# Decoding the second weight in the last batch's first product, and threshold and bias in two instructions

## The chip, the cores and the metric

The kernel runs on one core of a Trainium2 chip. The metric is the time of one execution on the device in microseconds (us), lower is better. The core has five engines that run side by side and wait for each other by semaphores: PE (matmul; its weight loads are shown apart as PEld), DVE (vector), ACT (scalar, activation), POOL (general) and SP, which here only issues DMAs. Each engine takes its instructions in order.

## The reference

Attention over 8 batches, 8 heads, 576 positions and a head width of 64, in which only scores within tau of their row's maximum count, followed by two matrix products with a gate between them:

```
scores = scale * (q @ k.T)                      # 8 x 8 x 576 x 576
thresh = max(scores, rows) - tau
scores = where(scores >= thresh, scores, -1e9)
attn   = exp(scores - max(scores)); attn = attn / (sum(attn) + 1e-9)
x      = (attn @ v) as (4608, 512)
h      = x @ w_in                               # 512 x 2048
g      = h * tanh(softplus(h))
out    = g @ w_out                              # 2048 x 512
```

q, k and v are 32-bit floats; w_in and w_out are 64-bit floats, and the host passes their words as they are. Turning the two 32-bit words of each number into one float32 is done on the chip and is called decoding here.

## The kernel before

**Decoding.** The class Decode (L112 to 146) takes a block of 128 rows and 256 columns. `load` (L121) fetches it with a DMA on SP, 256 KB. `first` (L124) is two ACT instructions that scale the upper and the lower words. `clamp`, `shift` (L131, L134) and the first half of `join` (L137) are three DVE instructions on 128x256 elements, and the second half of `join` is a POOL addition. The decoded number is then split for PE: `upper` (L142) rounds it to PE's fast float format on ACT, and `lower` (L145) subtracts the rounded part from the number, on DVE or POOL. Each weight has 32 such blocks.

**Attention loop.** One loop (L544) runs 288 steps and a few to drain; a step is one block of 128 query rows for one head (or 64 rows each of two heads). Its stages are spread over successive steps: PE computes scores s into PSUM; DVE takes the negated row maximum (`row_max`, L306); DVE computes two columns of the small tile st from it, the threshold st[:,1:2] = -nm - tau/scale and the bias st[:,2:3] = nm*scale (`exponential`, L313); ACT computes e = exp(scale*s + bias); DVE multiplies e by (s >= threshold) into p and sums its rows (`masked`, L322); in the next step POOL divides p by the sum (`normalise`, L337); PE transposes p into tp (and t), ACT copies the transposed block rounded to hi, DVE subtracts to get lo (`lo_main`, L375) and does the same for the short tail (tk); PE multiplies by the values. After every batch of 36 steps the first product's matmuls (`gemm1`, L455) of the batch before are woven into the steps, a listed number of matmuls per step (MIX, L62): each of 32 units is 12 matmuls of 288 columns into one of two PSUM buffers, a copy of the result h to a staging tile hst (by ACT, but by DVE in the last batch), and after every fourth unit a store to DRAM (hd). hst has two buffers. Within the first part of the program all instructions on PE, DVE, ACT and POOL keep the order in which they are written (class InOrder, L78); DMAs on SP and the second product's instructions are placed by the compiler's scheduler.

In `exponential` the first 39 steps (g < JOIN) write threshold and bias with two one-column instructions; from step 39 on they are one `scalar_tensor_tensor` on two columns, with the constant tiles turn and back (L162 to 168):

```
nc.vector.scalar_tensor_tensor(st[:, 1:3], turn, nm, back, ALU.mult, ALU.subtract)
```

Decoding rides in the loop as well (L617). The first weight's 32 blocks start at 12 of every 18 steps and end as split tiles in SBUF. The second weight's 32 blocks (`decode_w2`, L211) follow at 3 of every 18 steps (W2_STEPS); decoded but not split, each goes by a 128 KB DMA to a DRAM tile w2d.

**Last batch and second product.** When the attention's last steps are through, its SBUF is given back and the second part's tiles take its place (L645 on). The last batch's first product (384 matmuls) runs there. Written between its parts, w2d is read back in eight DMAs of 512 KB, ACT rounds each to hi and POOL subtracts to lo (`split_w2`, L674), and the first 256 columns of h are read, gated (`gate`, L666: ACT computes Mish, ACT rounds, POOL subtracts) and split. A part of the first weight's space is given back halfway (L714). Then the second product runs in ten chunks of the 4608 tokens, the first and the last of 256 columns and the rest of 512 (L747): for each chunk and each of four output blocks d, 48 matmuls o from g and the split second weight. The next chunk's h is loaded and gated by ACT and DVE (`make_g`, L730) while PE works on this one. The scheduler may put o matmuls of the first chunk between the last batch's h matmuls.

Of the kernel before, what the change touches and what calls it, by code (L numbers as in the profile page):

```python
# [14 lines left out]
P = 128  # L15
# [3 lines left out]
W1_STEPS = (1, 3, 4, 6, 7, 8, 10, 12, 13, 15, 16, 17)  # L19
W2_STEPS = (0, 12, 16)  # L20
STAGES = ((0, 1, 1), (0, 1, 1), (1, 2, 3))
THIRD = ((),)
# [15 lines left out]
NC = 512  # L38
# [35 lines left out]
def fv(ap):  # L74
    return ap.bitcast(F32)
# [36 lines left out]
class Decode:  # L112
# [24 lines left out]
    def join(self):  # L137
        nc, a, b, c = self.nc, self.a, self.b, self.c
        nc.vector.scalar_tensor_tensor(b, b, 0x80000000, a, ALU.bitwise_and, ALU.bitwise_or)
        nc.gpsimd.tensor_tensor(a, b, c, ALU.add)  # L140

# [7 lines left out]
def attention_moe(tc, q, k, v, tau, w_in, w_out, out):  # L149
# [3 lines left out]
    with ExitStack() as outer:  # L153
# [3 lines left out]
        hd = [dram.tile([P, NF, HB], F32, name=f"hd{i}") for i in range(NBLK)]  # L157
        w2d = dram.tile([P, NF, DM], F32, name="w2d")

        ident = cst.tile([P, P], F32, name="ident")  # L160
        make_identity(nc, ident)
        turn = cst.tile([P, 2], F32, name="turn")  # L162
        back = cst.tile([P, 2], F32, name="back")
        nc.sync.dma_start(back[:, 0:1], tau)
        nc.vector.memset(turn[:, 0:1], -1.0)
        nc.vector.memset(turn[:, 1:2], SCALE)
        nc.vector.memset(back[:, 1:2], 0.0)
        nc.vector.tensor_scalar(back[:, 0:1], back[:, 0:1], 1.0 / SCALE, None, ALU.mult)

        nc = Engines(tc)  # L170
        with ExitStack() as first:
# [6 lines left out]
            with ExitStack() as att:  # L178
# [17 lines left out]
                def decode_w1(d, j):  # L196
# [12 lines left out]
                    return [(work.first, skip), *spread(work, STAGES[(d + j) % 2]), *THIRD, *last]  # L209

                def decode_w2(f, j):  # L211
                    sl = slice(j * WC, (j + 1) * WC)
                    st = dec.tile([P, 4 * WC], U32, name="dec")
                    work = Decode(nc, st, None, None)
                    work.load(w_out[f * P:(f + 1) * P, sl])

                    def last():
                        nc.sync.dma_start(w2d[:, f, sl], fv(work.a))

                    return [(work.first, skip), *spread(work, STAGES[2]), (last,)]  # L220

# [90 lines left out]

                def exponential(s, st, e, apart):  # L313
                    nm = st[:, 0:1]
                    if apart:
                        nc.vector.tensor_scalar(st[:, 2:3], nm, SCALE, None, ALU.mult)
                        nc.vector.tensor_scalar(st[:, 1:2], nm, -1.0, back[:, 0:1], ALU.mult, ALU.subtract)
                    else:
                        nc.vector.scalar_tensor_tensor(st[:, 1:3], turn, nm, back, ALU.mult, ALU.subtract)
                    nc.scalar.activation(e, s[:, :, :HB], AF.Exp, bias=st[:, 2:3], scale=SCALE)  # L320
# [170 lines left out]
                weights = [lambda d=d, j=j: decode_w1(d, j) for j in range(DF // WC) for d in range(ND)]  # L491
                weights += [lambda f=f, j=j: decode_w2(f, j) for f in range(NF) for j in range(DM // WC)]
                decoding = []
# [50 lines left out]
                for g in range(NT + 5):  # L544
# [30 lines left out]
                    if g < NT:  # L575
                        exponential(tiles[g]["s"], tiles[g]["st"], tiles[g]["e"], g < JOIN)
                    if 3 <= g < NT + 3 and not full and ORDER[g % 2] == 1:
# [70 lines left out]

            def halves(pool, d):
                return [pool.tile([P, NF, P], F32R, name=f"w2{n}{d}") for n in "hl"]  # L650

            def slot(pool, shape, kind, n):

                return pool.tile(shape, kind, name="g", tag="g", bufs=n)

            def load_h(ht, c, fs):
# [13 lines left out]

            def load_w2(st, d, fs):
                nc.sync.dma_start(st, w2d[:, fs, d * P:(d + 1) * P])

            def split_w2(st, d, fs):  # L674
                hi, lo = w2[d]
                nc.scalar.copy(hi[:, fs], st)
                nc.gpsimd.tensor_tensor(lo[:, fs], st, fv(hi[:, fs]), ALU.subtract)

            def quarter(k):
                return slice(4 * k, 4 * k + 4)  # L680

            EIGHTS = (slice(0, 8), slice(8, 16))
            n0 = CHUNKS[1]
            w2 = [halves(wr, d) for d in range(2)]
            raw2 = slot(wr, [P, 2, NF, P], F32, 4)
            h0 = slot(wr, [P, NF, n0], F32, 4)
            g0 = [slot(wr, [P, NF, n0], F32R, 4) for _ in "hl"]
            for fs in EIGHTS:
                load_w2(raw2[:, 0, fs], 0, fs)
            for k in range(4):  # L690
                load_h(h0[:, quarter(k)], 0, quarter(k))
            for fs in EIGHTS:
                load_w2(raw2[:, 1, fs], 1, fs)
# [4 lines left out]
            advance(stream, 4 * UNIT)  # L698
            for fs in EIGHTS:
                split_w2(raw2[:, 0, fs], 0, fs)  # L700
            for k in range(4):
                gate(h0[:, quarter(k)], *(g[:, quarter(k)] for g in g0), nc.gpsimd)
            for fs in EIGHTS:
                split_w2(raw2[:, 1, fs], 1, fs)
            advance(stream, 4 * UNIT)
            raw2 = slot(wr, [P, 2, NF, P], F32, 4)
            for d in range(2):
                for fs in EIGHTS:
                    load_w2(raw2[:, d, fs], 2 + d, fs)
            h1 = slot(wr, [P, 8, NC], F32, 4)  # L710
            for k in range(2):
                load_h(h1[:, quarter(k)], 1, quarter(k))
            advance(stream, 8 * UNIT)
            early.close()  # L714
            er = second.enter_context(tc.tile_pool(name="er", bufs=1, side="right"))
            w2.append(halves(er, 2))
            for fs in EIGHTS:
                split_w2(raw2[:, 0, fs], 2, fs)
            for k in range(2):
                nc.scalar.activation(h1[:, quarter(k)], h1[:, quarter(k)], AF.Mish)  # L720
            for _ in stream:
# [3 lines left out]
        nc = tc.nc  # L725
        w2.append(halves(wl, 3))
        for fs in EIGHTS:
            split_w2(raw2[:, 1, fs], 3, fs)

        def make_g(c, q, pool, n):  # L730
            m = CHUNKS[c + 1] - CHUNKS[c]
            pair = slot(pool, [P, 2, 4, NC], F32R, n)
            gh, gl = pair[:, 0, :, :m], pair[:, 1, :, :m]
            for k in range(0, 4, 2):
                fs = slice(4 * q + k, 4 * q + k + 2)
                to = slice(k, k + 2)
                if c == 1 and q < 2:
                    nc.scalar.copy(gh[:, to], h1[:, fs])
                    nc.vector.tensor_tensor(gl[:, to], h1[:, fs], fv(gh[:, to]), ALU.subtract)
                else:  # L740
                    ht = wr.tile([P, 2, NC], F32, name="ht", bufs=2)
                    load_h(ht[:, :, :m], c, fs)
                    gate(ht[:, :, :m], gh[:, to], gl[:, to], nc.vector)
            return gh, gl

        ready = [[[g[:, quarter(q)] for g in g0] for q in range(4)]]
        for c in range(len(CHUNKS) - 1):  # L747
            m = CHUNKS[c + 1] - CHUNKS[c]
            if c + 2 < len(CHUNKS):
                homes = ((wl, 3),) * 3 + ((er, 1),) if c % 2 == 0 else ((wr, 4),) * 4  # L750
                ready.append([make_g(c + 1, q, *homes[q]) for q in range(4)])
            g = ready.pop(0)
            for d in range(ND):
                o = pso.tile([P, NC], F32, name="o")
                n = 0
                for f in range(NF):
                    wh, wlo = w2[d][0][:, f], w2[d][1][:, f]
# [53 lines left out]
```

## Time and profile before

| what | value |
|---|---|
| runs of the kernel | 1437.57, 1447.26 and 1449.11 us, median 1447.26 |
| profiled execution | 1436.91 us |
| its span in the profile | 1435.1 us |
| attention steps, first to last row maximum | 9.6 to 959.0 us |
| last batch's first product, to the second chunk's first matmul | 976.3 to 1054.8 us |
| second product after that | to about 1432 us |

A row of a group in the profile reads: line, engine, operation, output<-inputs, partitions x elements, count, then busy us and mean ns of one, then idle time of the engine ahead of it and what ended it. The line is that of the helper class (L88) for everything issued through InOrder, so instructions are told apart by their tiles. In the view by stretches each row has the stretch, its length, the busy us of each engine with its instruction count in brackets, the granted clock of PE as a share of full speed, the busy share of the DMA engines and GB/s. In the view of the waits a row has who waited for whom, the total us, the number of waits and the longest. In the view in order of time a row has start, length, engine, line, operation and tiles, and in square brackets the idle time ahead. In the views of one tile, three numbers with slashes are the minimum, median and maximum in ns.

### The profile page before, as it was taken

Reading aid. Unit: us, or ns where it says so; the run is one execution under the profiler, and the core shown is the slowest. Engines: PE = TensorE matmul, PEld = TensorE weight load, DVE = VectorE, ACT = ScalarE, POOL = GpSimd, SP = SyncE. Lnnn points to the kernel's source line nnn. Section 1 sums busy time; section 2 is a strip of 40 time slices with the busy share of each in tenths; the row PEclk is TensorE's granted clock in tenths of the full one; section 3 lists DMA queues with packets and bytes.
Section 4 is the critical chain, followed back from the end, with each engine's and each line's share of the span. In section 5 each row is a group of like instructions: output and inputs, shape, how many; then the busy total and the mean of one; then the engine's idle time right before and its main releaser. Section 6 shows DMA issues by size and latency. Waiting matters only on the chain.

```text
span 1435.1 us, 27051 instructions
## 1 busy us (share of the span) xinstructions
PE 1380.3 (96%) x8798; PEld 1228.5 (86%) x8798; DVE 1035.1 (72%) x2730; ACT 936.6 (65%) x2072; POOL 783.7 (55%) x1099
## 2 busy tenths in 40 slices
PE   8998899999999999999999999999999999999999
PEld 5555889899898998989899899998988888888888
DVE  5999999999999999999999999981243322322210
ACT  5888788787887888878788788874255434433310
POOL 4778887778777787877878778756110000000000
PEclk8999999999999999999999999999999999999999
DMA  4334333433333333333333333217545434534210
GB/s 139 100 98 118 116 118 104 139 95 120 114 109 130 104 120 106 112 118 109 122 109 104 97 106 102 92 51 216 181 126 155 138 105 139 137 99 126 87 52 30
DMA packets 134525, 162.98 MB, mean 114 GB/s; under 512 B 23793, under 2 KB 113905, under 8 KB 134385
## 3 DMA queue, kind: packets, MB, share of 16 engines
q1 hardware_dynamic: 134384, 161.26, 37.0%
q8 instruction: 70, 1.15, 0.3%
q14 instruction: 71, 0.57, 0.1%
HBM read 109.84 MB, written 51.38 MB: 112 GB/s over the span
## 4 chain that ended last, share of the span: by engine, by line
PE 68%; DVE 18%; ACT 5%; issue 5%; DMA 2%; POOL 1%; SPq 1%; DVEq 0%; ACTq 0%; POOLq 0%
PE o L760 26%; PE h L88 16%; PE s L88 11%; PE y L88 10%; DVE st L88 7%; PE tp L88 5%; DVE p L88 5%; DVE dec L88 2%; ACT e L88 2%; DVE lo L88 2%; DVE tk L88 1%; PE t L88 1%; DMA hd<-hst 1%; POOL g L88 1%; ACT x L88 1%
## 5 line engine op out<-in xcount | busy, mean ns | idle before, releaser
L760 PE MATMUL o<-g,w2h 128*128 128x512 f32 (+1 forms) x1280 | 365.0, 370 | 0.9 <-DVE g L669 0.7
L88 PE MATMUL h<-xh,w1h 128*128 128x288 f32 x1024 | 303.7, 297 | 3.3 <-DVE hst L88 2.4
L88 PE MATMUL h<-xl,w1h 128*128 128x288 f32 x1024 | 303.4, 296 | 0.5 <-POOL xl L88 0.5
L88 PE MATMUL h<-xh,w1l 128*128 128x288 f32 x1024 | 303.3, 296 | 0.0
L88 PE MATMUL s<-k,q 128*128 128x288 f32 (+1 forms) x1280 | 259.4, 328 | 41.7 <-DVE p L88 37.8
L88 ACT ACTIVATE e<-s,st 128x576 f32<-128x576 f32 x288 | 214.0, 743 | 128.5 <-DVE st L88 125.8
L88 POOL TENSOR_SCALAR p<-p,st 128x576 f32<-128x576 f32 x288 | 245.3, 852 | 75.2 <-DVE st L88 56.2
L760 PEld LDWEIGHTS o<-g,w2h 128*128 128x128 f32 x1280 | 231.9, 188 | 44.8 <-DVE g L669 1.1
L88 PEld LDWEIGHTS s<-k,q 128*128 128x128 f32 (+1 forms) x1280 | 183.9, 191 | 94.9 <-DVE p L88 74.8
L88 DVE SCALAR_TENSOR_TENSOR p<-s,st,e 128x576 f32<-128x576 f32 x288 | 234.8, 815 | 30.3 <-ACT e L88 24.6
L760 PE MATMUL o<-g,w2l 128*128 128x512 f32 (+1 forms) x640 | 236.7, 370 | 0.0
L88 DVE TENSOR_REDUCE st<-s 128x1 f32<-128x576 f32 x288 | 216.3, 751 | 7.3 <-PE s L88 7.2
L88 PEld LDWEIGHTS h<-xh,w1h 128*128 128x128 f32 x1024 | 193.8, 189 | 4.0 <-DVE hst L88 2.8
L88 PEld LDWEIGHTS h<-xl,w1h 128*128 128x128 f32 x1024 | 193.9, 189 | 0.7 <-POOL xl L88 0.7
L88 PEld LDWEIGHTS h<-xh,w1l 128*128 128x128 f32 x1024 | 193.6, 189 | 0.0
L669 DVE TENSOR_TENSOR g<-ht,g 128x1024 fp32r<-128x1024 f32 (+1 forms) x68 | 78.4, 1162 | 155.6 <-ACT g L668 155.6
L88 DVE TENSOR_TENSOR lo<-tp,hi 128x512 fp32r<-128x512 f32 (+1 forms) x280 | 171.2, 620 | 13.8 <-ACT hi L88 13.1
L88 PE MATMUL tp<-ident,p 128*128 128x128 f32 x1152 | 174.9, 274 | 3.8 <-DVE lo L88 1.3
L88 ACT CAST hi<-tp 128x512 fp32r<-128x512 f32 (+1 forms) x280 | 150.5, 548 | 16.3 <-PE tp L88 12.9
L667 ACT ACTIVATE ht<-ht 128x1024 f32<-128x1024 f32 (+1 forms) x68 | 68.7, 1010 | 132.1 <-DMA ht<-hd 128.6
L88 PEld LDWEIGHTS tp<-ident,p 128*128 128x128 f32 x1152 | 138.8, 141 | 13.9 <-issue 6.9
L88 POOL TENSOR_TENSOR x<-x,yo 64x256 f32<-64x256 f32 (+1 forms) x112 | 90.2, 806 | 89.8 <-ACT yo L88 88.0
(64 smaller groups left out, 2265.0 us busy)
## 6 DMA issues: line engine op xcount, KB each, us to landing
hd<-hst SPq DMA_DIRECT2D x64, 576.0 KB, 3.3
r<-q SPq DMA_DIRECT2D x120, 160.0 KB, 2.3
r<-k SPq DMA_DIRECT2D x120, 160.0 KB, 2.3
ht<-hd SPq DMA_DIRECT2D x60, 288.0 KB, 3.3
r<-v SPq DMA_DIRECT2D x56, 160.0 KB, 2.3
dec<-w_in SPq DMA_DIRECT2D x32, 256.0 KB, 2.8
dec<-w_out SPq DMA_DIRECT2D x32, 256.0 KB, 2.8
out_t<-ost SPq DMA_DIRECT2D x32, 256.0 KB, 2.8
```

What stands on the lines that cost most here:

```text
L88: made = method(*args, **kwargs)
L667: nc.scalar.activation(ht, ht, AF.Mish)
L669: engine.tensor_tensor(gl, ht, fv(gh), ALU.subtract)
L760: nc.tensor.matmul(o[:, :m], a, b, start=n == 0, stop=n == 3 * NF - 1)
```

## The change

The second weight is no longer decoded in the attention loop, and w2d is gone. Its 32 blocks are fetched, decoded and split in the last batch's stage, one step of a small pipeline ahead of each of the 32 units of 12 matmuls: at unit u, ACT's `first` of block u-3; ACT's `upper` of block u-5; DVE's `clamp`, `shift` and `sign` and POOL's `add` (the two halves of `join`) of block u-4; and `lower` of block u-5, on DVE for odd blocks and on POOL for even ones, after which the buffer fetches block u+1. There are six buffers, four in a slot of the large tiles and two that the second product later uses for h. The split weight is held as two halves of 256 output columns instead of four of 128. The first chunk's four gates come at units 9, 11, 13 and 15. The second chunk's h, of which half was loaded and put through Mish in this stage, is loaded at unit 18 and gated wholly in `make_g`. The tiles for g are four slots each in two pools, in place of three, one and four in three pools.

In the loop, threshold and bias are two one-column instructions in every step, the bias first; the tile turn and the second column of back go.

```diff
-W2_STEPS = (0, 12, 16)
...
     def join(self):
-        nc.vector.scalar_tensor_tensor(b, b, 0x80000000, a, ALU.bitwise_and, ALU.bitwise_or)
-        nc.gpsimd.tensor_tensor(a, b, c, ALU.add)
+        self.sign()
+        self.add()
...
-                def exponential(s, st, e, apart):
+                def exponential(s, st, e):
                     nm = st[:, 0:1]
-                    if apart:
-                        nc.vector.tensor_scalar(st[:, 2:3], nm, SCALE, None, ALU.mult)
-                        nc.vector.tensor_scalar(st[:, 1:2], nm, -1.0, back[:, 0:1], ALU.mult, ALU.subtract)
-                    else:
-                        nc.vector.scalar_tensor_tensor(st[:, 1:3], turn, nm, back, ALU.mult, ALU.subtract)
+                    nc.vector.tensor_scalar(st[:, 2:3], nm, SCALE, None, ALU.mult)
+                    nc.vector.tensor_scalar(st[:, 1:2], nm, -1.0, back, ALU.mult, ALU.subtract)
...
-                weights += [lambda f=f, j=j: decode_w2(f, j) for f in range(NF) for j in range(DM // WC)]
...
-                    if weights and (g % 18 in W1_STEPS if len(weights) > 32 else g % 18 in W2_STEPS):
+                    if weights and g % 18 in W1_STEPS:
...
+            def fetch(i):
+                if i < 2 * NF:
+                    st = four[:, i % 6] if i % 6 < 4 else small(U32, [P, 4 * WC])
+                    work[i] = Decode(nc, st, None, None)
+                    j, f = divmod(i, NF)
+                    work[i].load(w_out[f * P:(f + 1) * P, j * WC:(j + 1) * WC])
+
+            def decode_step(u):
+
+                if (i := u - 3) in work:
+                    work[i].first()
+                if (i := u - 5) in work:
+                    j, f = divmod(i, NF)
+                    work[i].hi, work[i].lo = (w[:, f] for w in w2[j])
+                    work[i].upper()
+                if (i := u - 4) in work:
+                    work[i].clamp()
+                    work[i].shift()
+                    work[i].sign()
+                    work[i].add()
+                if (i := u - 5) in work:
+                    work.pop(i).lower(nc.vector if i % 2 else nc.gpsimd)
+                    fetch(i + 6)
...
+            for u in range(NF * 2):
+                if u == NF + 2:
+                    early.close()
+                    er = second.enter_context(tc.tile_pool(name="er", bufs=1, side="right"))
+                    w2.append(weights2(er, 1))
+                decode_step(u)
+                if u in (9, 11, 13, 15):
+                    k = (u - 9) // 2
+                    gate(h0[:, quarter(k)], *(g[:, quarter(k)] for g in g0), nc.gpsimd)
+                if u == NF + 2:
+                    h1 = slot(wr, [P, 8, NC], F32, 4)
+                    for k in range(2):
+                        load_h(h1[:, quarter(k)], 1, quarter(k))
+                advance(stream, UNIT)
+            for u in range(NF * 2, NF * 2 + 5):
+                decode_step(u)
```

More of the change, by code (lines that the diff above doesn't have):

```diff
@@ L19 @@
 W1_STEPS = (1, 3, 4, 6, 7, 8, 10, 12, 13, 15, 16, 17)
-W2_STEPS = (0, 12, 16)
-STAGES = ((0, 1, 1), (0, 1, 1), (1, 2, 3))
+STAGES = ((0, 1, 1), (0, 1, 1))
 THIRD = ((),)
@@ L137, in join, with sign, add @@
     def join(self):
-        nc, a, b, c = self.nc, self.a, self.b, self.c
-        nc.vector.scalar_tensor_tensor(b, b, 0x80000000, a, ALU.bitwise_and, ALU.bitwise_or)
-        nc.gpsimd.tensor_tensor(a, b, c, ALU.add)
+        self.sign()
+        self.add()
+    def sign(self):
+        self.nc.vector.scalar_tensor_tensor(self.b, self.b, 0x80000000, self.a, ALU.bitwise_and, ALU.bitwise_or)
+    def add(self):
+        self.nc.gpsimd.tensor_tensor(self.a, self.b, self.c, ALU.add)
     def upper(self):
@@ L157, in attention_moe @@
         hd = [dram.tile([P, NF, HB], F32, name=f"hd{i}") for i in range(NBLK)]
-        w2d = dram.tile([P, NF, DM], F32, name="w2d")
         ident = cst.tile([P, P], F32, name="ident")
         make_identity(nc, ident)
[L162 to L168, printed above, removed]
+        back = cst.tile([P, 1], F32, name="back")
+        nc.sync.dma_start(back, tau)
+        nc.vector.tensor_scalar(back, back, 1.0 / SCALE, None, ALU.mult)
         nc = Engines(tc)
@@ L209, in decode_w1 @@
                     return [(work.first, skip), *spread(work, STAGES[(d + j) % 2]), *THIRD, *last]
[L211 to L220, printed above, removed]
                 def prep(pi):
@@ L575, in attention_moe @@
                     if g < NT:
-                        exponential(tiles[g]["s"], tiles[g]["st"], tiles[g]["e"], g < JOIN)
+                        exponential(tiles[g]["s"], tiles[g]["st"], tiles[g]["e"])
                     if 3 <= g < NT + 3 and not full and ORDER[g % 2] == 1:
@@ L647, in attention_moe, with small @@
             pso = second.enter_context(tc.tile_pool(name="pso", bufs=4, space=PSUM))
-            def halves(pool, d):
-                return [pool.tile([P, NF, P], F32R, name=f"w2{n}{d}") for n in "hl"]
             def slot(pool, shape, kind, n):
                 return pool.tile(shape, kind, name="g", tag="g", bufs=n)
+            def small(kind, shape):
+                return wr.tile(shape, kind, name="ht", tag="ht", bufs=2)
             def load_h(ht, c, fs):
@@ L669, in gate, with weights2 @@
                 engine.tensor_tensor(gl, ht, fv(gh), ALU.subtract)
[L671 to L677, printed above, removed]
             def quarter(k):
                 return slice(4 * k, 4 * k + 4)
-            EIGHTS = (slice(0, 8), slice(8, 16))
+            def weights2(pool, j):
+                return [pool.tile([P, NF, WC], F32R, name=f"w2{n}{j}") for n in "hl"]
             n0 = CHUNKS[1]
-            w2 = [halves(wr, d) for d in range(2)]
-            raw2 = slot(wr, [P, 2, NF, P], F32, 4)
+            w2 = [weights2(wr, 0)]
+            four = slot(wr, [P, 4, 4 * WC], U32, 4)
             h0 = slot(wr, [P, NF, n0], F32, 4)
             g0 = [slot(wr, [P, NF, n0], F32R, 4) for _ in "hl"]
-            for fs in EIGHTS:
-                load_w2(raw2[:, 0, fs], 0, fs)
+            work = {}
+            def fetch(i):
[19 more added lines that the diff above has]
+                    fetch(i + 6)
+            for i in range(6):
+                fetch(i)
             for k in range(4):
                 load_h(h0[:, quarter(k)], 0, quarter(k))
-            for fs in EIGHTS:
-                load_w2(raw2[:, 1, fs], 1, fs)
             for _ in stream:
@@ L697, in attention_moe @@
             UNIT = 12
[L698 to L720, printed above, removed]
+            for u in range(NF * 2):
[14 more added lines that the diff above has]
+                decode_step(u)
             for _ in stream:
@@ L725, in attention_moe, with make_g @@
         nc = tc.nc
[L726 to L730, printed above, removed]
+        def make_g(c, q, pool):
             m = CHUNKS[c + 1] - CHUNKS[c]
-            pair = slot(pool, [P, 2, 4, NC], F32R, n)
+            pair = slot(pool, [P, 2, 4, NC], F32R, 4)
             gh, gl = pair[:, 0, :, :m], pair[:, 1, :, :m]
@@ L737, in make_g @@
                 if c == 1 and q < 2:
-                    nc.scalar.copy(gh[:, to], h1[:, fs])
-                    nc.vector.tensor_tensor(gl[:, to], h1[:, fs], fv(gh[:, to]), ALU.subtract)
+                    gate(h1[:, fs], gh[:, to], gl[:, to], nc.vector)
                 else:
-                    ht = wr.tile([P, 2, NC], F32, name="ht", bufs=2)
+                    ht = small(F32, [P, 2, NC])
                     load_h(ht[:, :, :m], c, fs)
@@ L749, in attention_moe @@
             if c + 2 < len(CHUNKS):
-                homes = ((wl, 3),) * 3 + ((er, 1),) if c % 2 == 0 else ((wr, 4),) * 4
-                ready.append([make_g(c + 1, q, *homes[q]) for q in range(4)])
+                ready.append([make_g(c + 1, q, (wl, wr)[c % 2]) for q in range(4)])
             g = ready.pop(0)
@@ L755, in attention_moe @@
                 n = 0
+                j, at = divmod(d * P, WC)
                 for f in range(NF):
-                    wh, wlo = w2[d][0][:, f], w2[d][1][:, f]
+                    wh, wlo = (w[:, f, at:at + P] for w in w2[j])
                     gh, gl = (x[:, f % 4] for x in g[f // 4])
```

## The prediction

> **What bounds the kernel now.** I read the page first, then the stretches, then the waits inside them. The page:
>
> ```profile
> span 1435.1 us, 27051 instructions
> PE 1380.3 (96%) x8798; PEld 1228.5 (86%) x8798; DVE 1035.1 (72%) x2730; ACT 936.6 (65%) x2072; POOL 783.7 (55%) x1099
> PE 68%; DVE 18%; ACT 5%; issue 5%; DMA 2%; POOL 1%; SPq 1%; DVEq 0%; ACTq 0%; POOLq 0%
> ```
>
> PE looks full everywhere, but the chain of waits gives DVE 18% of the span, so somewhere PE waits for DVE. The stores of the decoded second weight say where its decode lies:
>
> ```profile
> L218 SPq DMA_DIRECT2D w2d<-dec x32: 326/327/425, 208.2 to 820.5; - x32
> ```
>
> I cut the span by that. The view by stretches, for tile e alone, has one ACT instruction per attention step, so its second count (behind ACT's busy time) is the number of steps. The fence after it is the same view for all engines, in the order PE, weight loads, DVE, ACT, POOL, then clock, DMA share and GB/s:
>
> ```profile
> 126.60:186.20 59.60, 12.42 (x32) 11.16 (x15) 0.91 0.40 116
> 186.20:849.70 663.50, 162.97 (x396) 147.22 (x198) 1.00 0.36 113
> 849.70:959.00 109.30, 28.84 (x71) 26.04 (x35) 1.00 0.26 85
> ```
>
> ```profile
> 186.20:849.70 663.50, 633.09 (x4668) 602.81 (x4667) 638.69 (x1727) 535.72 (x1319) 526.32 (x782) 1.00 0.36 113
> 849.70:959.00 109.30, 108.93 (x832) 106.85 (x831) 103.28 (x290) 89.97 (x216) 80.86 (x125) 1.00 0.26 85
> 976.30:1054.80 78.50, 75.36 (x567) 74.54 (x568) 23.52 (x39) 29.39 (x28) 30.98 (x14) 0.98 0.60 185
> ```
>
> A step takes 663.5/198 = 3.351 us while the second weight is decoded and 109.3/35 = 3.123 us just after, with the same matmuls per step (4668/198 = 23.6, 832/35 = 23.8). PE idles 4.6% of the first stretch and 0.3% of the second. What the weight loads wait for, in the same two stretches:
>
> ```profile
> PEld s L88 <- DVE p L88: 58.2, 119, 1.1
> ...
> PEld s L88 <- DVE p L88: 2.2, 8, 0.4
> ```
>
> Taking these waits out gives (663.5 - 58.2)/198 = 3.057 and (109.3 - 2.2)/35 = 3.060. So a step that never waits for DVE would cost PE 3.06 us; DVE bounds the stretch with decode, PE nearly bounds the one without. After the attention the last batch's product runs on PE alone with DVE, ACT and POOL mostly idle (last row).
>
> **Threshold and bias.** The group that goes, with its mean in ns, and the spread (minimum, median, maximum in ns) of it and of the two one-column forms, which the kernel has in its first steps:
>
> ```profile
> L88 DVE SCALAR_TENSOR_TENSOR st<-turn,st,back 128x2 f32<-128x2 f32 x249 | 119.4, 479 | 0.0
> ...
> L88 DVE SCALAR_TENSOR_TENSOR st<-turn,st,back x249: 210/368/926, 127.4 to 959.8; 128x2 f32<-128x2 f32 x125
> L88 DVE TENSOR_SCALAR st<-st x381: 134/144/155, 10.4 to 961.8; 128x1 f32<-128x1 f32 x191
> L88 DVE TENSOR_SCALAR st<-st,back x39: 201/204/207, 10.5 to 124.3; 128x1 f32<-128x1 f32 x39
> ```
>
> Two columns cost 479 ns on average but 210 at best, so most of it is a stall. The instructions in order of time show on what:
>
> ```profile
> 859.54 0.87 POOL L88 TENSOR_TENSOR x<-x,yo 64x320 f32<-64x320 f32 x1 [1.40 <-ACT yo L88]
> 860.06 0.37 DVE L88 SCALAR_TENSOR_TENSOR st<-turn,st,back 128x2 f32<-128x2 f32 x1
> ...
> 861.66 0.83 POOL L88 TENSOR_SCALAR p<-p,st 128x576 f32<-128x576 f32 x1
> 862.84 0.22 DVE L88 SCALAR_TENSOR_TENSOR st<-turn,st,back 128x2 f32<-128x2 f32 x1
> ```
>
> The first ends at 860.43 with POOL's instruction (860.41); the second, with POOL idle since 862.49, takes 0.22. The one-column forms never exceed 155 and 207 ns in 381 and 39 cases, so they don't stall so. The pair is 144 + 204 = 348 ns against 479, a gain of 0.13 us a step, 33 us over 249 steps if DVE were the bound throughout. DVE instructions also overlap their neighbours by some 0.08 (below, the reduce lasts until 81.07 and the next begins at 80.99), short ones most: two sums and the pair together take 81.30 - 80.99 = 0.31.
>
> ```profile
> 80.32 0.75 DVE L88 TENSOR_REDUCE st<-s 128x1 f32<-128x576 f32 x1
> 80.99 0.27 DVE L88 TENSOR_SCALAR st<-st 128x1 f32<-128x1 f32 x3
> 81.30 0.15 DVE L88 RECIPROCAL st<-st 128x1 f32<-128x1 f32 x1
> ```
>
> That puts the pair near 0.18 and the gain near 0.2. As a range for the edit: a loss of 0.14 (0.35 - 0.21) if the stall only moves to a neighbour, to a gain of 0.2; nearest is the case of the first steps, where the pair stands in the same place, so I take the gain. The bias also comes first, so e on ACT starts earlier.
>
> [...]
>
> **The second weight out of the loop.** What one decode costs each engine in the loop, from the groups by line:
>
> ```profile
> L88 DVE TENSOR_SCALAR dec<-dec 128x256 f32<-128x256 f32 x64 | 33.1, 518 | 0.0
> L88 DVE TENSOR_SCALAR dec<-dec 128x256 uint32<-128x256 uint32 x64 | 25.1, 392 | 0.5
> L88 DVE SCALAR_TENSOR_TENSOR dec<-dec 128x256 uint32<-128x256 uint32 x64 | 44.7, 698 | 0.7
> L88 ACT ACTIVATE dec<-dec 128x256 uint32<-128x256 uint32 x64 | 28.1, 439 | 0.0
> L88 POOL TENSOR_TENSOR dec<-dec 128x256 uint32<-128x256 uint32 x64 | 48.0, 751 | 2.3 <-DVE dec L88 1.4
> L88 POOL TENSOR_TENSOR w1l<-dec,w1h 128x256 fp32r<-128x256 f32 x23 | 17.5, 763 | 2.9 <-ACT w1h L88 2.6
> ```
>
> Per decode the loop loses 0.52 + 0.39 + 0.70 = 1.61 us on DVE, two ACT instructions of 0.44, 0.75 on POOL, and on SP a load and a store. 32 x 1.61 = 51 us of DVE plus the 33 above is 84 us, but PE allows no step under 3.06. So the loop can fall to between 3.06 and 3.123 us; I take 3.09, as PE's work varies from step to step. Terms: 198 x (3.351 - 3.09) = 51.7; 35 x (3.123 - 3.09) = 1.2; and in the 15 steps before 186.2, where the first weight still keeps DVE busy, 15 x 0.2 = 3. **Loop: -56 us**, between -45 (3.123, nothing else) and -63 (3.06 in 233 steps and the 3).
>
> **The same work in the last batch.** Before, the stage runs from the last batch's first h matmul to the first 512-column o, the 78.5 us from 976.3 to 1054.8 in the third row above. Its pace, its first load, and what the moved work costs when nothing stalls it (minimum first):
>
> ```profile
> 1021.03 0.46 DVE L88 COPY hst<-h 128x288 f32<-128x288 f32 x1 [1.14 <-PE h L88]
> 1040.20 0.46 DVE L88 COPY hst<-h 128x288 f32<-128x288 f32 x1 [1.14 <-PE h L88]
> 1041.00:1051.00 10.00, 10.00 (x87) 10.00 (x86) 1.00 0.23 85
> 977.96 1.00 SPq L672 DMA_DIRECT2D g<-w2d  x2
> dec<-w_out SPq DMA_DIRECT2D x32, 256.0 KB, 2.8
> L88 POOL TENSOR_TENSOR g<-g 128x1024 fp32r<-128x1024 f32 x4 | 9.4, 2394 | 1.3 <-ACT g L88 1.3
> L88 DVE TENSOR_SCALAR dec<-dec x128: 272/386/966, 24.0 to 813.3; 128x256 f32<-128x256 f32 x64, 128x256 uint32<-128x256 uint32 x64
> L88 DVE SCALAR_TENSOR_TENSOR dec<-dec x64: 414/710/2307, 26.9 to 817.4; 128x256 uint32<-128x256 uint32 x64
> L88 DVE TENSOR_TENSOR w1l<-dec,w1h x9: 409/412/956, 50.9 to 141.0; 128x256 fp32r<-128x256 f32 x9
> ```
>
> PE needs (1040.20 - 1021.03)/12 = 1.60 us per unit of 12 matmuls, 51 us for 32 units, and 10/87, about 0.12 us, for each of the first chunk's 192 o matmuls (23 us). Now every unit also carries one decode, ahead of the copy of h on DVE, which is in order: a late decode holds the copy, the copy holds one of two PSUM buffers, and PE stops. DVE alone would need, at the short durations 0.27 + 0.27 + 0.41 and half of 0.41, plus 0.46 for the copy, 1.6 us: just PE's pace. But the stalls above tie DVE's SBUF instructions to POOL's. If one runs at a time, a pair of units holds 4 x 0.27 + 2 x 0.41 + 0.41 on DVE and 2 x 0.75 + 0.76 on POOL, 4.6 us, less some overlap, about 4.3; the copies from PSUM hide under POOL. So 2.15 us per unit, and four gate subtractions on POOL (2.39 each) add 9.6.
>
> [...]
>
> The stage's first load can issue when the attention's buffers are free (977.96), lands 2.8 later, ACT converts (0.87), so decoding starts about 6.5 us into the stage. Unit 31 carries decode 27: 6.5 + 28 x 2.15 + 9.6 = 76.3; the last four decodes end under the 23 us of o matmuls that follow, some 3 us of which fit into the gaps before. 76.3 + 23 - 3 = 96.3 against 78.5: **+18 us**. Bounds: PE's pace 1.6 and no gaps, 51 + 23 + 2 = 76, so -2; and nothing side by side, (4.6 + 0.92)/2 = 2.8 per unit, 6.5 + 78 + 9.6 + 23 = 117, so +39. Chunk 1's gates, later on ACT than before, I put at +2. The stores to and loads from w2d, the POOL splits and their waits go, but they lay beside PE's work, and I count them as nothing; if uncovered they would add at most the 3 us by which 78.5 exceeds PE's 75.4.
>
> **Sum.** The profiled execution took 1436.9, 1.8 beyond its span. 1436.9 - 56 + 18 + 2 = 1401. The three runs shown lie between 1437.57 and 1449.11 with the median 10 above the profiled one; I add half of that: **1406 us**.
>
> **Rivals.** (1) The last batch hides the decode: +0 for +18 and +2; 1436.9 - 56 + 5 = 1386. For it: DVE 30% busy there now. Against it: the stalls. 13%. (2) Two instructions cost more than one and the stall moves on: +0.14 on DVE a step. The stretch without decode then goes to 3.123 + 0.14 = 3.26, the loop gains 198 x 0.09 - 50 x 0.14 = 11, and 1436.9 - 11 + 20 + 5 = 1451, no change. For it: 210 ns at best. Against it: 155 ns at most for a one-column form. [...] 10%. (3) The loop ends between, near 3.2, because with less work in front of it p waits for e: 198 x 0.15 + 3 = 33, 1436.9 - 33 + 20 + 5 = 1429. For it: such waits exist; against it: they are small, and e now starts earlier. 12%.
>
> ```profile
> DVE p L88 <- ACT e L88: 24.6, 85, 1.4
> ```
>
> (4) Slower: in the last batch SP is one queue for loads of the weight and stores of h. A load waits until its buffer's decode is done, the store behind it waits too, and h's two staging buffers stop DVE, which stops the decode. DVE has such waits now:
>
> ```profile
> DVE hst L88 <- DMA hd<-hst: 15.2, 2, 8.3
> ```
>
> With 7 waits of 8.3 us it costs 58 more: 1401 + 58 + 5 = 1464; it decides from 5 us per store (36 in all). Against it: loads are six decodes ahead, 13 us against 2.8. 7%.
>
> **Chances and range.** My case 58%, with its own range 1388 to 1424; rivals as given. The bounds of the terms span 1436.9 - 63 - 2 = 1372 to 1436.9 - 45 + 41 = 1433. Range 1383 to 1436: it takes in (1) and (3), cuts the corner where every term is at its best, and leaves out (2) and (4). Measurements of this kernel tell about 1% from no change: 58 + 13 + most of (3) make faster 0.82, (2) and the rest same 0.11, (4) slower 0.07.
>
> **What would show it.** Steps of 3.06 to 3.12 us from 186 on, PE's waits for DVE p under 10 us; the one-column pair at 143 and 204 ns; the last batch's copies of h some 2.2 us apart instead of 1.6, DVE and POOL stalled in turn, the stage near 96 us. Wrong: steps above 3.2 (2 or 3), copies at 1.6 (1), or h's copies waiting for stores (4).

## The result, and the profile after

The changed kernel took 1400.47 us (median of 4 runs, 1396.20 to 1407.83) against 1442.41 us for the kernel before (4 runs, 1435.35 to 1449.11). The ratio is 0.9715, with a 95% interval of 0.9644 to 0.9786: faster by 2.9%, some 41 us. Executions of one kernel lie up to 14 us apart here. The profiled execution took 1407.83 us, the slowest of the four. The lines of its page that answer to those shown for the kernel before:

```profile
span 1406.0 us, 27557 instructions
PE 1370.3 (97%) x8798; PEld 1234.7 (88%) x8798; DVE 1008.2 (72%) x2992; ACT 947.1 (67%) x2098; POOL 774.1 (55%) x1107
PE 88%; DVE 5%; ACT 3%; DMA 2%; issue 2%; POOL 0%; SPq 0%; POOLq 0%; ACTq 0%; DVEq 0%
```

PE's share of the busy time moved from 96% to 97%, which says little. The chain of waits says more: PE went from 68% to 88% of the span, DVE from 18% to 5%. The view by stretches, cut at the same steps as before: first for tile e (the second count is the number of steps), then for all engines.

```profile
134.80:195.20 60.40, 12.42 (x32) 11.18 (x15) 0.92 0.35 104
195.20:803.70 608.50, 163.22 (x396) 147.54 (x198) 1.00 0.33 103
803.70:911.40 107.70, 28.88 (x72) 26.07 (x35) 1.00 0.27 87
```

```profile
195.20:803.70 608.50, 608.42 (x4667) 599.97 (x4668) 560.30 (x1829) 520.06 (x1252) 496.52 (x749) 1.00 0.33 103
803.70:911.40 107.70, 107.69 (x835) 106.83 (x833) 99.66 (x327) 89.94 (x216) 80.95 (x125) 1.00 0.27 87
928.70:1026.40 97.70, 83.31 (x567) 80.67 (x568) 79.82 (x153) 55.07 (x118) 50.65 (x54) 0.91 0.62 199
```

A step of the 198 now takes 608.5/198 = 3.073 us and PE is busy in all of it; in the 35 after them it takes 3.077. The waits of PE's weight loads for p, in the same two stretches, were 58.2 and 2.2 us:

```profile
PEld s L87 <- DVE p L87: 8.7, 34, 1.9
...
PEld s L87 <- DVE p L87: 0.8, 4, 0.2
```

Where the 29.1 us between the two profiled spans lie, stretch by stretch:

| stretch | before | after | difference | forecast |
|---|---|---|---|---|
| up to step 39 | 126.6 | 134.8 | +8.2 | 0 |
| 15 steps with the last of the first weight | 59.6 | 60.4 | +0.8 | -3 |
| 198 steps | 663.5 | 608.5 | -55.0 | -51.7 |
| 35 steps | 109.3 | 107.7 | -1.6 | -1.2 |
| last row maximum to the start of the last batch's stage | 17.3 | 17.3 | 0 | 0 |
| the last batch's stage | 78.5 | 97.7 | +19.2 | +18 |
| rest of the second product | 380.3 | 379.6 | -0.7 | +2 |

The first 39 steps are written the same in both kernels. Their difference belongs to the execution: PE's granted clock in the first 50 us was 0.90 in the one and 0.76 in the other (rows in the last section), and in the kernels of the experiments that share these steps they ended between 125.9 us (clock 0.93) and 138.4 us (0.66). Without the first row the difference is 37.3 us.

A note on the cut of the stage: the h matmul at 976.3 is not the last batch's first. Nine h matmuls of it stand up to 2.3 us earlier, ahead of a wait for the last xh. The cut lies at the same matmul in every kernel here, so the differences hold.

### The profile page after: what moved, and what is told of

It reads as the page before. It is cut to its first block, busy times and chain, and to the rows that moved or that the text cites. A ratio compares the mean times of both kernels' runs of the same rounds, so it can differ in the third digit from the quotient of the medians.

```text
span 1406.0 us, 27557 instructions
## 1 busy us (share of the span) xinstructions
PE 1370.3 (97%) x8798; PEld 1234.7 (88%) x8798; DVE 1008.2 (72%) x2992; ACT 947.1 (67%) x2098; POOL 774.1 (55%) x1107
## 4 chain that ended last, share of the span: by engine, by line
PE 88%; DVE 5%; ACT 3%; DMA 2%; issue 2%; POOL 0%; SPq 0%; POOLq 0%; ACTq 0%; DVEq 0%
PE o L751 27%; PE h L87 25%; PE s L87 14%; PE y L87 12%; PE tp L87 9%; PE t L87 1%; DVE g L87 1%; DVE st L87 1%; DVE p L87 1%; DVE ht L87 1%; DVE dec L87 1%; DMA g<-hd 1%; DMA g<-w_out 1%; ACT e L87 1%; DVE hst L87 0%
## 5 line engine op out<-in xcount | busy, mean ns | idle before, releaser
L87 ACT ACTIVATE e<-s,st 128x576 f32<-128x576 f32 x288 | 214.4, 744 | 36.1 <-DVE st L87 29.0
L87 DVE TENSOR_TENSOR lo<-tp,hi 128x512 fp32r<-128x512 f32 (+1 forms) x280 | 174.7, 632 | 50.7 <-ACT hi L87 43.8
L751 PEld LDWEIGHTS o<-g,w2l 128*128 128x128 f32 x640 | 121.9, 191 | 25.9 <-POOL w2l L87 3.9
```

Of the source, the lines that this page charges most:

```text
L87: made = method(*args, **kwargs)
```

## The experiments

Times are ratios to the kernel before on the same chip, with 95% intervals; stages are from each one's profile, from that h matmul to the first 512-column o. A stage is one execution: the same code of the stage took 97.7 us in the changed kernel, and 96.4 and 95.2 us in the two experiments that leave it as it is. Differences of up to some 2.5 us between two stages show nothing by themselves.

**Moving the decode alone.** The changed kernel with the two-column instruction from step 39 on, as before.

```diff
+                    if apart:
                         nc.vector.tensor_scalar(st[:, 2:3], nm, SCALE, None, ALU.mult)
                         nc.vector.tensor_scalar(st[:, 1:2], nm, -1.0, back[:, 0:1], ALU.mult, ALU.subtract)
+                    else:
+                        nc.vector.scalar_tensor_tensor(st[:, 1:3], turn, nm, back, ALU.mult, ALU.subtract)
```

> The decode of the second weight is moved as in the change, but threshold and bias stay one two-column instruction from step 39 on. Theory (PE's own 3.06 us per step is the bound once the decode is out of the loop, the two-column instruction only adds what its stalls make PE wait): steps as in the stretch without decode of the kernel before, 3.12 us, against 3.077 in the changed kernel, so 233 x 0.045 = 10 us slower than the changed kernel and about 28 us faster than before; the last batch's stage 97 to 98 us as in the changed kernel. Rival (DVE is still the bound and every stall of that instruction is paid, 0.2 us a step): steps 3.28, 46 us slower than the changed kernel, slower than before.

Measured: 1414.69 us, ratio 0.9832 (0.9789 to 0.9876). The 198 and 35 steps, by tile e, and the stage:

```profile
185.30:805.90 620.60, 163.46 (x396) 147.19 (x198) 1.00 0.33 101
805.90:915.10 109.20, 28.82 (x71) 26.03 (x35) 1.00 0.26 85
...
932.40:1028.80 96.40, 81.03 (x567) 78.00 (x568) 79.86 (x153) 55.13 (x119) 50.64 (x54) 0.95 0.61 200
```

Steps of 620.6/198 = 3.134 us, near the 3.123 of the stretch without decode before, and the stage about as long as in the changed kernel. The theory holds: DVE no longer adds its whole stall to a step, and the two-column instruction costs 0.06 us a step. The move by itself is worth 1.7%.

**Two instructions alone.** The kernel before with the two one-column instructions in every step; the decode stays in the loop.

```diff
-                    if apart:
...
-                    else:
-                        nc.vector.scalar_tensor_tensor(st[:, 1:3], turn, nm, back, ALU.mult, ALU.subtract)
```

> Only threshold and bias become two one-column instructions; the second weight is decoded in the loop as before. Theory (DVE bounds the steps with decode, and the pair takes about 0.2 us a step off it; PE's 3.06 is the floor): steps with decode 3.351 - 0.2 = 3.15, those without 3.08, so 198 x 0.2 + 35 x 0.04 = 41 us less in the loop and nothing more in the last batch: 36 to 41 us faster than before, as much as the whole change. Rival (the decode itself, not the two-column instruction, is what makes PE wait): the loop gains only the 0.045 us a step that the stretch without decode gained, 10 us.

Measured: 1405.85 us, ratio 0.9757 (0.9722 to 0.9792). By tile e, the stage, and the wait of PE's weight loads in the 198 steps:

```profile
197.40:824.80 627.40, 163.04 (x396) 147.20 (x198) 1.00 0.38 119
824.80:932.40 107.60, 28.87 (x72) 26.06 (x35) 1.00 0.27 87
...
949.70:1027.20 77.50, 73.50 (x568) 72.88 (x569) 23.41 (x39) 29.31 (x28) 31.04 (x14) 1.00 0.60 187
...
PEld s L88 <- DVE p L88: 22.4, 79, 0.7
```

Steps with decode take 627.4/198 = 3.169 us: 0.18 less than before, near the 0.2 of the theory. Not all of it need be DVE's own time. In these steps DVE waited 11.7 us for e in the kernel before and not at all here, as the bias no longer comes out of a stalled instruction (its waits for hi rose from 3.5 to 16.8 us). How much that makes of the 36.1 us was not tried apart. Most of the gain needs no move of the decode. Given the two instructions, the move takes 627.4 - 608.5 = 18.9 us out of the loop and adds 97.7 - 77.5 = 20.2 us to the last batch; the intervals of this kernel and of the whole change overlap. The gains don't add: the move alone gives 1.7%, the pair alone 2.4%, both 2.9%, because both take DVE time out of the same steps, and together they come to 3.07 us, where PE is busy all the time.

**One two-column instruction with one tensor input.** The changed kernel, with threshold and bias together again, but not as a two-tensor instruction.

```diff
-                    nc.vector.tensor_scalar(st[:, 2:3], nm, SCALE, None, ALU.mult)
-                    nc.vector.tensor_scalar(st[:, 1:2], nm, -1.0, back, ALU.mult, ALU.subtract)
+                    nc.vector.tensor_scalar(st[:, 1:3], turn, nm, back, ALU.mult, ALU.subtract)
```

> The changed kernel with threshold and bias in one instruction again, two columns, but with a single SBUF tensor as input and both other operands as per-partition scalars (the bias is lower by the same constant in every row, which the division by the sum takes out). Theory (the two-column instruction stalled because it has two tensor inputs in SBUF): about 0.2 us without stalls, steps 3.07 to 3.08, as the changed kernel. [...]

Measured: 1426.06 us, ratio 0.9896 (0.9856 to 0.9936). The group, its spread, and the 198 steps by tile e:

```profile
L87 DVE TENSOR_SCALAR st<-turn,st,back 128x2 f32<-128x2 f32 x288 | 132.8, 461 | 0.0
...
L87 DVE TENSOR_SCALAR st<-turn,st,back x288: 279/377/1649, 9.4 to 932.8; 128x2 f32<-128x2 f32 x144
...
199.30:822.70 623.40, 163.42 (x395) 147.31 (x198) 1.00 0.32 101
...
301.77 0.83 POOL L87 TENSOR_SCALAR p<-p,st 128x576 f32<-128x576 f32 x1
302.21 0.41 DVE L87 TENSOR_SCALAR st<-turn,st,back 128x2 f32<-128x2 f32 x1
...
949.40:1044.60 95.20, 81.85 (x567) 79.21 (x568) 79.83 (x153) 54.94 (x118) 50.67 (x54) 0.93 0.61 199
```

The theory falls: the instruction stalls as the one with two tensor inputs did (461 ns on average against 479), and steps take 3.148 us instead of 3.07 to 3.08. The two rows in order of time show it end with POOL's instruction (302.62 and 302.60). Counted over the traces, 162 of its 288 took over 320 ns, and each of these ended within 60 ns of a POOL instruction; of the kernel before's 249, 146 took over 300 ns, and 145 of them ended so. The changed kernel's 918 one-column instructions on st never took more than 209 ns, though POOL was at work when more than 740 of them began.

So the stall doesn't need the second tensor input, and in these kernels the one-column instructions avoid it. Instructions with two SBUF inputs were held as well: of the kernel before's 64 sign instructions of the decode, which have two, 50 took over 450 ns, and all 50 ended 265 to 286 ns after a POOL instruction. Whether two columns or two tensor inputs held the two-column instruction in the kernel before is not shown, and no run shows why one column escapes.

The steps after the first weight are not the whole loss. These 233 steps take 16.5 us more than in the changed kernel, but the time is 26 us longer. The first 39 steps have the instruction here too (435 ns on average) and ended at 138.2 us; how much of that is the instruction and how much the start's clock, 0.80 in the first 50 us, the run doesn't show.

**Subtractions to DVE in the last batch.**

```diff
-                    work.pop(i).lower(nc.vector if i % 2 else nc.gpsimd)
+                    work.pop(i).lower(nc.vector)
...
-                    gate(h0[:, quarter(k)], *(g[:, quarter(k)] for g in g0), nc.gpsimd)
+                    gate(h0[:, quarter(k)], *(g[:, quarter(k)] for g in g0), nc.vector)
```

> The changed kernel, but in the last batch all 32 subtractions of lower and the four of the gates go to DVE, which does them in 0.41 and 1.22 us against POOL's 0.76 and 2.40. Theory (DVE's and POOL's SBUF instructions exclude each other, so what counts is their sum): per pair of units 0.35 us less, 16 x 0.35 = 6, and 4 x 1.2 = 5 for the gates: the stage 87 us instead of 97.8, the kernel 10 us faster than the changed one. Rival (DVE alone is the bound there, POOL runs beside it): DVE gets 16 x 0.41 + 4 x 1.22 = 11 us more, the stage 109 us.

Measured: 1395.03 us, ratio 0.9685 (0.9647 to 0.9724); the stage

```profile
928.80:1017.10 88.30, 79.81 (x567) 76.42 (x568) 69.94 (x171) 53.73 (x117) 27.18 (x34) 0.96 0.64 212
...
990.60 0.45 DVE L87 COPY hst<-h 128x288 f32<-128x288 f32 x1
992.49 0.45 DVE L87 COPY hst<-h 128x288 f32<-128x288 f32 x1
```

88.3 us, 7 to 9 less than the three executions with these subtractions on POOL, as the theory of exclusion has it, and far from the rival's 109. DVE got 18 instructions more and was busy 69.9 us instead of 79.8: the same 96 instructions of clamp, shift and sign took 54.2 us in the changed kernel and 38.1 here, as fewer POOL instructions stood in their way. A unit in the steady part takes 1.89 us. In the whole time the gain can't be told: the interval of the ratio overlaps with that of the changed kernel.

**All decode instructions to DVE.** On top of the kernel before this one.

```diff
-                    work[i].add()
+                    nc.vector.tensor_tensor(work[i].a, work[i].b, work[i].c, ALU.add)
```

> [...] POOL does nothing in the last batch's stage. Theory (exclusion): DVE has 0.2 + 0.2 + 0.34 + 0.34 + 0.34 + 0.46 = 1.9 us per unit and waits for no one, the clamp and shift always take 0.27 us: units of 1.9, the gates 1.2 each, the stage 84 to 86 us. Rival (DVE alone is the bound): 32 x 0.4 us more than the kernel with lower and gates on DVE, the stage 13 us longer than there.

Measured: 1391.39 us, ratio 0.9655 (0.9611 to 0.9699). One unit of DVE in order of time, and the stage:

```profile
984.70 0.45 DVE L87 COPY hst<-h 128x288 f32<-128x288 f32 x1
985.07 0.61 DVE L87 TENSOR_SCALAR g<-g 128x256 f32<-128x256 f32 x2
985.72 0.42 DVE L87 SCALAR_TENSOR_TENSOR g<-g 128x256 uint32<-128x256 uint32 x1
986.17 0.43 DVE L87 CUSTOM_DVE_ANT_0 g<-g 128x512 uint16<-128x512 uint16 x1
986.52 0.42 DVE L87 TENSOR_TENSOR w2l<-g,w2h 128x256 fp32r<-128x256 f32 x1
986.85 0.45 DVE L87 COPY hst<-h 128x288 f32<-128x288 f32 x1
...
925.80:1007.00 81.20, 75.37 (x553) 73.31 (x553) 68.47 (x190) 47.21 (x110) 1.53 (x2) 0.98 0.64 214
```

The decode's DVE instructions stall no more: clamp and shift take 0.61 together, and each of the 64 took 280 to 297 ns. The addition runs as a custom instruction on 512 half-words, here of 0.43 us. The unit is 2.15 us, not 1.9, longer than the 1.89 of the kernel before this one, and still the stage is shorter, 81.2 us. The rows count 553 matmuls here and 567 there: the first 512-column o now comes ahead of the first chunk's last 14 matmuls, so the like stage is some 1.7 us longer, about 82.9 (14 at 0.12 us, an estimate from the rate of o matmuls before).

The stage thus isn't set by the unit alone. The last h matmul starts 73.4 us into the stage there and 73.9 here, but counted in order of time, 122 instead of 91 of the first chunk's o matmuls now stand ahead of it, where PE would idle, and fewer remain behind it. Both theory and rival missed that. That this count decides is not shown: the spread kernel below has only 67 ahead and a stage no longer than that with 91.

**Gates spread over ACT; everything one unit earlier; then all of it on DVE.** Three kernels, each on top of the one with the subtractions on DVE: Mish and rounding of a gate in successive units; also every decode one unit earlier; also the addition on DVE.

```diff
+                if u in (9, 11, 13, 15):
+                    k = (u - 9) // 2
+                    nc.scalar.activation(h0[:, quarter(k)], h0[:, quarter(k)], AF.Mish)
+                if u in (10, 12, 14, 16):
+                    k = (u - 10) // 2
+                    nc.scalar.copy(g0[0][:, quarter(k)], h0[:, quarter(k)])
+                    nc.vector.tensor_tensor(g0[1][:, quarter(k)], h0[:, quarter(k)], fv(g0[0][:, quarter(k)]), ALU.subtract)
...
-                if (i := u - 3) in work:
+                if (i := u - 2) in work:
...
-                if (i := u - 4) in work:
+                if (i := u - 3) in work:
```

> The kernel with lower and gates on DVE, and each gate's rounding and subtraction one unit after its Mish, so that ACT's work is spread over eight units. Theory (in the four gate units ACT sets the pace: 0.87 + 0.40 + 1.06 + 1.05 = 3.4 us, and the waits behind it make 4.2): units 9 to 16 take 2.4 each on average instead of 3.0, 4 to 5 us less in the stage, 83 to 84 us against 88.3. Rival (those units wait for the loads of h and for the store of h, not for ACT): no change.

> As the kernel with spread gates, and every decode one unit earlier: first of block u-2, clamp to add of block u-3, upper and lower of block u-4. Theory (the stage ends where the last decodes end plus the matmuls that use them): one unit less, 1.9 us, 82 us. Rival (ACT then waits for the first load and the chain starts no earlier): the same as with spread gates.

> The kernel with spread and earlier gates and decodes, and the decode's addition on DVE as well, so that POOL does nothing in the last batch's stage. Theory (what counts is how much of PE's idle time between the h matmuls is filled: with all work on DVE units were 2.15 us against 1.88 with the addition on POOL, but 122 instead of 91 o matmuls of the first chunk stood ahead of the last h, and the stage was 81 against 88): the stage 78 to 80 us, the kernel 5 us faster than with the addition on POOL, about 1384. Rival (DVE's time per unit sets the stage): 28 x 0.27 = 7.5 us more than the 85.6 with the addition on POOL, 93.

Measured, in this order: 1394.19 us, ratio 0.9669 (0.9625 to 0.9713); 1387.89 us, 0.9644 (0.9606 to 0.9683); 1387.65 us, 0.9649 (0.9605 to 0.9694). The stages:

```profile
931.40:1018.40 87.00, 78.29 (x567) 73.95 (x568) 73.27 (x173) 54.29 (x118) 27.22 (x34) 1.00 0.65 217
...
919.00:1004.60 85.60, 79.52 (x567) 75.45 (x568) 71.53 (x173) 54.35 (x118) 27.04 (x34) 0.98 0.67 220
...
919.40:1001.30 81.90, 75.97 (x559) 72.91 (x560) 71.18 (x196) 48.70 (x113) 1.55 (x2) 1.00 0.67 219
```

Spreading gave 1.3 us instead of 4 to 5: that part of the theory falls. One unit earlier gave 1.4 of 1.9. Neither is more than two executions of one stage differ by, and the granted clocks differ too (0.96, 1.00, 0.98), so neither gain is shown. The third reached 81.9 us (559 matmuls, so about 82.9 for the like stage), neither the 78 to 80 of its theory nor the 93 of its rival, no shorter than with all work on DVE alone, and no time that can be told from the second.

The last two are 3.5 to 3.6% faster than the kernel before. Their intervals still overlap with that of the changed kernel (0.9644 to 0.9786); that they beat it too rests on their stage, at least 9.6 us shorter than in its three executions. Which of these versions is best lies within their intervals.

**The last batch without the decode's bit work.** This kernel leaves out clamp, shift, sign and addition of the second weight, so it computes something else.

```diff
-                    work[i].clamp()
-                    work[i].shift()
-                    work[i].sign()
-                    work[i].add()
```

> The changed kernel without clamp, shift, sign and add in the last batch: the second weight is not decoded there, only loaded, scaled, rounded and split, so the output is not the reference's. Theory (DVE's and POOL's decode instructions stretch the units): units fall to PE's 1.6 us, the stage to between 78 and 82 us with the gates on POOL. Rival (loads of the weight and stores of h queue on SP and set the pace): the stage stays above 90.

Measured: 1387.19 us, ratio 0.9627 (0.9577 to 0.9677); the stage

```profile
919.30:1000.80 81.50, 75.54 (x567) 74.53 (x568) 33.87 (x57) 52.89 (x118) 23.59 (x22) 0.98 0.72 237
```

Without the four instructions the stage is 81.5 us, 16.2 less than the 97.7 (13.7 less than the shortest of the three executions), and the copies of h in the steady part come 1.60 us apart. So the loads and stores on SP do not set the pace of a unit. They still stop it in places: here ACT waits 19.2 us in eight waits for loads of the weight, and DVE 4.3 us in one for a store of h. The 81.5 is close to what the kernels with all work on DVE reach with the decode in.

## Why the prediction was right

The time (1406 forecast, 1400.5 measured) came out by the two mechanisms of the forecast, a loop that falls to PE's floor and a last batch in which DVE and POOL take turns. The forecast change was 36 us; the profiled spans without their first row give 37.3. The medians differ by 42 us; the 5 us that no term explains lie within the spread of the executions. Inside the two sums, sizes cancelled, as the last point says.

**PE's floor.** The steps went from 3.351 to 3.073 us, between the 3.06 and 3.123 that were given, nearer the floor than the 3.09 chosen: 3.3 us more gain than forecast in the 198 steps. Moving the decode alone gave nearly the pace of the stretch without decode (3.134), and the pair took the rest. The floor was read from the right row: the waits of the weight loads, 58.2 us. PE's own idle time in the 198 steps before was only 30.4 us, which would have put the floor at 633.09/198 = 3.197, and the steps went below that. So the busy time of PE held slack that only the waits of its weight loads show. By the same sum the changed kernel's floor would be (608.5 - 8.7)/198 = 3.03, so that 3.07 is PE's very limit is not shown.

**The pair.** It runs at 145 and 204 ns (medians), without stalls:

```profile
L87 DVE TENSOR_SCALAR st<-st x630: 132/145/157, 9.6 to 914.0; 128x1 f32<-128x1 f32 x158
L87 DVE TENSOR_SCALAR st<-st,back x288: 201/204/209, 9.7 to 912.2; 128x1 f32<-128x1 f32 x144
```

The 0.2 us a step held where DVE is the bound and its neighbours read PSUM (the row maximum, at most 758 ns in all 288 steps of the changed kernel) or single columns (at most 209 ns): 0.18 with the decode in the loop. Rival 2 did not come: with one instruction more per step, the kernel with that edit alone is 2.4% faster, since what counted was not how many instructions there were but which could stall.

The prediction has POOL idle since 862.49 in its example without a stall. A POOL instruction of 0.22 us on st follows there and ends at 862.68; the two-column instruction begins at 862.84, so the reading stands.

**The step that failed: -3 us in the 15 steps with the first weight.** They took 0.8 us more. In the other executions with the pair the same steps took 58.8 to 60.3 us, five times 59.4 or 59.5, and their 30 DVE instructions on the decode tile 16.6 to 18.5 us, so there was neither the gain of 3 nor a sure loss. All DVE, ACT and POOL instructions on the decode tile in these steps, in the kernel before, in the one that only moves the decode, and in the changed one:

```profile
126.60:186.20 59.60, 15.08 (x30) 10.18 (x26) 14.71 (x20) 0.91 0.40 116
...
126.50:185.30 58.80, 15.43 (x30) 10.22 (x26) 14.68 (x20) 0.94 0.35 104
...
134.80:195.20 60.40, 18.09 (x30) 10.17 (x26) 15.21 (x20) 0.92 0.35 104
```

The same 30 DVE instructions took 18.09 us instead of 15.08 as soon as the two-column instruction no longer waited ahead of them: 3.0 us, just what the pair was to save in 15 steps. Here the stall moved to the next instruction that can stall, the case that the prediction gave as the low end of the range for the edit. It is not so everywhere: in the 198 steps with the second weight's decode, the pair alone took 36.1 us off. The prediction took the first steps as the nearest case; it should have asked which stalling instructions follow in each stretch.

**The last batch.** The stage took 97.7 us; 96.3 were forecast, and 78.5 before. Copies of h in the steady part:

```profile
999.75 0.45 DVE L87 COPY hst<-h 128x288 f32<-128x288 f32 x1
1001.28 0.45 DVE L87 COPY hst<-h 128x288 f32<-128x288 f32 x1
1003.86 0.45 DVE L87 COPY hst<-h 128x288 f32<-128x288 f32 x1
...
942.65 0.75 POOL L87 TENSOR_TENSOR g<-g 128x256 uint32<-128x256 uint32 x1 [1.08 <-ACT w2h L87]
943.36 0.79 POOL L87 TENSOR_TENSOR w2l<-g,w2h 128x256 fp32r<-128x256 f32 x1
942.80 1.50 DVE L87 TENSOR_SCALAR ht<-ht 128x256 f32<-128x256 f32 x2
```

A pair of units takes 1003.86 - 999.75 = 4.11 us, 2.06 a unit (forecast 2.15). The last three rows show why: DVE's clamp and shift take 1.50 us beside two POOL instructions, against 0.61 with POOL idle. In the whole stage 41 of the 64 took over 330 ns, and all 41 ended 147 to 158 ns after a POOL instruction: they wait until POOL is done. The rest of the sum held less exactly. The last decodes did not end wholly under the o matmuls, the store of h did stop DVE, but once, and in the same 10 us a load of the weight came late:

```profile
PE o L751 <- POOL w2l L87: 3.7, 1, 3.7
...
DVE hst L87 <- DMA hd<-hst: 2.3, 1, 2.3
...
DVE p L87 <- ACT e L87: 0.4, 1, 0.4
...
947.99 0.77 ACT L87 ACTIVATE g<-g 128x256 f32<-128x256 f32 x2 [4.15 <-DMA g<-w_out]
940.00:950.00 10.00, 6.75 (x44) 6.28 (x43) 7.40 (x19) 3.88 (x10) 4.23 (x7) 0.92 0.94 342
```

That is rival 4 at 2.3 us for the store and 4.15 for the load, partly at the same time, in place of 58; the DMA engines were busy for 0.94 of those 10 us. Rival 1 needed POOL out of the way, and even then the stage was 81 to 83, not 78. Rival 3 did not come: p waited for e only once in the 198 steps, 0.4 us (the row of DVE p).

**The sizes that cancelled.** Loop -55.8 (forecast -56) and stage +19.2 (+18) look right by themselves, but each holds two misses that cancel, and that is luck. In the loop, the 15 steps gave 3.8 us too little and the other steps 3.7 too much. In the stage, the decode began 6.7 us in (forecast 6.5, though the terms listed for it add up to 5.3), and the last copy of h came at 76.7 us (76.3). Between them lie 28 units of 2.06 us and four gates at some 2.1 us each, 66 us against the forecast 69.8; the other 4 us are about what the waits for the store and the late load took, which the sum did not have. The +2 for the second chunk's gates was -0.7.

## What to carry to other kernels

Before a task is moved off a busy engine, ask what else slows that engine in the same steps: a stall removed from one small instruction gave most of this gain without moving anything, and with it the move paid nothing that can be told (18.9 us out of the loop, 20.2 us into the last batch). Read the floor from a stretch where the suspected work is already absent, and from the waits of PE's weight loads rather than from PE's idle time; it told here to a few us how far either edit could go. And where the trace shows one engine's instructions held until another's end, as clamp and shift were here by POOL (41 of 64), count the sum of both engines' instructions, and give the work to the one that does it in less time, even if that one looks like the bound; here that took 7 to 9 us off the stage.

## What the runs showed of the hardware that was not expected

One DVE instruction on two columns stalled behind POOL, with one tensor input (162 of 288) as with two (145 of 249), and the instructions on one column never did (none of 918 above 209 ns). The counts stand with the experiment on the single tensor input.

PE's granted clock was either 1.00 or 0.50 in the records of these traces. In the changed kernel's last-batch stage it was 0.50 four times, each beginning within 1 us of the end of a gap of 1.9 to 3.7 us between matmuls. In the first, PE stood still for 3.07 us until 947.93; from 948.5 on it had half clock for 3.4 us, with PE busy all the time. The four stretches, 17 us in all, make the 0.91 of the stage. From the last batch on, all the profiled executions together have 23 gaps of 1.7 to 3.8 us; half clock came behind 16 of them, and why not behind the other 7 was not tried.

The first 50 us differ from execution to execution. Below are the stretch behind the gap, then the first 50 us and the stretch at half clock in them, for the changed kernel and for the kernel before.

```profile
948.50:951.90 3.40, 3.40 (x16) 3.40 (x15) 2.50 (x5) 3.34 (x5) 1.47 (x2) 0.50 0.24 88
...
0.00:50.00 50.00, 43.84 (x171) 28.92 (x172) 26.06 (x105) 24.44 (x57) 21.66 (x31) 0.76 0.37 108
13.20:37.10 23.90, 22.91 (x64) 14.05 (x65) 12.60 (x52) 9.45 (x23) 9.60 (x12) 0.50 0.29 89
...
0.00:50.00 50.00, 44.09 (x208) 29.49 (x208) 33.85 (x132) 30.29 (x71) 27.52 (x38) 0.90 0.43 121
8.20:18.40 10.20, 7.65 (x29) 6.40 (x29) 6.63 (x27) 3.65 (x8) 3.27 (x5) 0.50 0.86 264
```

In the same 50 us 171 matmuls got done in the one and 208 in the other, and half clock lasted 23.9 us in the one and 10.2 in the other. Half of that difference is 6.9 us, an estimate of what it cost, near the 8.2 of the first row of the table. What decides how long it lasts at the start was not tried.
